# Pooled attention and a four-expert feed-forward in one kernel: weight loads by halves, four weight sums on GpSimd, one copy on ScalarE

## The chip, the core and the metric

The kernel runs on one core of one Trainium2 chip. A core has TensorE (PE, with its weight loads PEld), VectorE (DVE), ScalarE (ACT), GpSimd (POOL) and SyncE (SP), and 16 DMA engines. The metric is the device time of one execution in microseconds, the median over runs.

## The reference

Inputs are in float32: q, k and v (8 batches, 8 heads, 576 tokens, 64 channels), probabilities of 4 experts for each of 8 x 576 = 4608 tokens, and the experts' weights w1 (4 x 512 x 1024) and w2 (4 x 1024 x 512).

```python
k_p = k.reshape(B, H, 72, 8, D).mean(axis=3)      # keys and values averaged over 8 tokens
v_p = v.reshape(B, H, 72, 8, D).mean(axis=3)
attn = softmax(q @ k_p.T / sqrt(D))
x = (attn @ v_p) as (4608, 512)                   # heads side by side
p = probs / (probs.sum(-1) + 1e-9)
out = sum over e of p[:, e] * (relu(x @ w1[e]) @ w2[e])
```

Nearly all arithmetic is in the two products of each expert.

## The kernel before

**Chunks.** The tokens are cut into nine chunks of 512: the first 512 tokens of each batch, and a last chunk of the remaining 64 tokens of all eight. For each chunk the attention gives a turned input xT (512 channels by 512 tokens, bf16); then each expert has an up-product with w1, a relu into a hidden tile H, and a down-product with w2, whose parts are scaled by the probability and added to acc.

**Seven products for eight.** Most products are done by a scheme of seven block products with sums of blocks (Strassen's, in Winograd's form). `up_product(c, e, unit, step)` (L680, matmuls L698) does step 0 to 6 of an up-product for one of two units of columns, `down(c, e, step)` (L749, matmuls L766) a step of a down-product. They need sums of weight blocks, made once for each expert: `first_weight_sums(e)` gives four of w1 (three into the tile wu, one in place into w1's own tile), `weight_sums(e)` four of w2 (three into the tile wt, one in place). Each is one `combine` (L249, a tensor_tensor on VectorE over 128 x 1024 bf16 elements). Sums over a chunk's input are `x_sum` (tile xs and one in place), over its hidden tile `hidden_sums` (tiles S2, S3 and in place). Relu sums from PSUM (L678), evictions into acc (L842) and copies (L711, L713, L774 on ScalarE) drain the banks.

**The first chunk** is written out by hand in `first_chunk`, since weights are still arriving. Expert 0 is done first, expert 1's up-product plainly, and expert 1's and 2's down-products plainly by `down_plain` (L787, matmuls L792): for one block of 128 tokens eight matmuls of 128 x 512, the eight chunks of w2's rows in order, then one eviction. Between them stands the attention of chunk 1: `queries_of_two` turns queries on PE into a bank and copies them out (L374), `keys` does so for keys (L304, L306), `scores_of_two` makes scores (L388) and exponents (L399, L413), `values_folds` sums value rows on VectorE into vp (L275, L338), `context` multiplies by vp (L463) and divides (L424, L425), `turn` turns the result (L481, L483). `context` goes through the heads in order, and vp is filled by two halves of heads.

**Order.** Each engine runs its instructions in the order in which the program lists them, and waits on semaphores. Loads with a change of type from float32 to bf16 are issued from GpSimd's queue (`nc.gpsimd.dma_start`), in program order: after the first keys and values, w1 of experts 0 and 1, the probabilities, w1 of 2, w2 of 0, w1 of 3, keys, queries, w2 of 1, values, w2 of 2, and, inside `first_chunk`, w2 of 3 (which waits until its room, used for partial sums, is free) and the keys, queries and values of chunk 2 (`load_wide`, `load_q`, `load_q_rem`). The software queue has eight semaphores in turn, so a load is issued when the load eight places before it has landed.

The loads of the weights are these:

```python
def load_w1(e):
    n = 2 if e == 0 else 1          # column halves
def load_w2(e):
    n = 2 if e in (0, 2) else 1     # row halves
```

**From chunk 1 on** a loop over slots g takes one step of an up-product and one of the down-product of the expert before in each slot, with attention pieces of later chunks at listed slots. In its first slots the down-product is that of chunk 0 and expert 3, which uses wt of expert 3 from step 2 on. One part in seven of the down-products is added to acc on GpSimd (`POOLED`, L780, a tensor_tensor over 128 x 512 float32); otherwise GpSimd does no arithmetic after the start.

Of the kernel before, what the change touches and what calls it, by code (L numbers as in the profile page):

```python
# [10 lines left out]
ALU = mybir.AluOpType  # L11
# [6 lines left out]
def kernel(  # L18
# [10 lines left out]
    nc = tc.nc  # L29

    B, H, S, D = q.shape
    E, DM, F = moe_w1.shape
# [7 lines left out]
    KC = DM // P  # L40
# [16 lines left out]
    HF, HN, HD, HK = FCH // 2, NT // 2, DM // 2, KC // 2  # L57
# [9 lines left out]
    chains = [psum.tile([P, NT], F32, name=f"o_ps{i}") for i in range(2)]  # L67
# [81 lines left out]
    def rows_of(src, b, lo, hi):  # L149
        return src[b].rearrange("h (j r) d -> j h r d", r=POOL)[:, :, lo:hi, :]  # L150
# [13 lines left out]
    def load_wide(what, part):  # L164
        src, raw, wide = ((k, raw_k, wide_k), (v, raw_v, wide_v))[what]
        n = wide.shape[2]
        if part == 0:
            nc.gpsimd.dma_start(out=wide, in_=rows_of(src, BUSY, 0, n))
        else:
            n += 2 * (part - 1)  # L170
            nc.gpsimd.dma_start(out=raw[:], in_=rows_of(src, BUSY, n, n + 2),
                                accum_op=ALU.add if part > 1 else ALU.bypass)
# [30 lines left out]
        )  # L203

    def load_w1(e):
        n = 2 if e == 0 else 1
        for i in range(n):
            fs = slice(i * F // n, (i + 1) * F // n)

            for ks in [slice(0, HK), slice(HK, KC)] if n == 2 and i == 0 else [slice(0, KC)]:  # L210
                nc.gpsimd.dma_start(  # L211
                    out=w1_bf[:, e, ks, fs],
                    in_=moe_w1[e][:, fs].rearrange("(kc p) f -> p kc f", p=P)[:, ks],
                )

    def load_w2(e):
        n = 2 if e in (0, 2) else 1
        for i in range(n):
            fcs = slice(i * FCH // n, (i + 1) * FCH // n)
            nc.gpsimd.dma_start(  # L220
                out=w2_bf[:, e, fcs], in_=moe_w2[e].rearrange("(fc p) d -> p fc d", p=P)[:, fcs]
            )
# [23 lines left out]
            in1=inv[:].unsqueeze(2).to_broadcast([P, NBLK, E]), op=ALU.mult,  # L246
        )

    def combine(dst, a, op, b):  # L249
        nc.vector.tensor_tensor(out=dst, in0=a, in1=b, op=op)  # L250

    state = {}
    turns = {"spare": 0, "work": 0, "att": 0, "up": 0}
# [109 lines left out]
    def queries_of_two(pair, bank, copy):  # L363

        q_sb = raws[("q", 1)]
        if pair == 0:
            state[("qT", 1)] = apool.tile([P, H, 2, P], BF16, name="qT")
        qt_ps = bank.bitcast(BF16)[:, 0:8 * P].rearrange("p (h a t) -> p h a t", h=4, a=2)
        for hh in range(4):
            for rr in range(2):  # L370
                nc.tensor.transpose(
                    qt_ps[:, hh, rr, :], q_sb[:, 2 * pair + hh, 2 * rr:2 * rr + 2, :], ident[:]
                )
        copy(out=state[("qT", 1)][:, 2 * pair:2 * pair + 4], in_=qt_ps)  # L374
# [18 lines left out]
    def scores(b, pair, part=None):  # L393
        sc_ps = two_banks(b)
        if part != 1:
            score_products(b, pair, [sc_ps[:, r2] for r2 in range(2)])
        if part == 0:
            return
        nc.scalar.activation(  # L399
            out=state[("expT", b)][:, 2 * pair:2 * pair + 2].rearrange("j h a b t -> j b (h a) t"),  # L400
            in_=sc_ps[0:SP].rearrange("j b (h t) -> j b h t", t=P),
            func=ACT.Exp, scale=EXP_SCALE,
        )

    def scores_of_two(b, pair, bank=1):

        scores(b, pair, 0 if b > 1 else None)
        banks = [unit[bank][:] for unit in units]  # L410
        score_products(b, pair + 1, banks)
        for r2 in range(2):
            nc.scalar.activation(  # L413
                out=state[("expT", b)][:, 2 * pair + 2:2 * pair + 4, :, r2].rearrange("j h a t -> j (h a) t"),
                in_=banks[r2][0:SP].rearrange("j (h t) -> j h t", t=P),
                func=ACT.Exp, scale=EXP_SCALE,
            )
# [227 lines left out]
        w = w1_bf[:, e]  # L645
        return w[:, 0:HK, 0:FH], w[:, HK:KC, 0:FH], w[:, 0:HK, FH:F], w[:, HK:KC, FH:F]

    def first_weight_sums(e):
        b11, b21, b12, b22 = weight_parts(e)
        t = wu_bf[:, e]  # L650
        return [lambda: combine(t[:, 0], b12, ALU.subtract, b11),
                lambda: combine(t[:, 1], b22, ALU.subtract, t[:, 0]),
                lambda: combine(t[:, 2], b21, ALU.subtract, t[:, 1]),
                lambda: combine(b12, b22, ALU.subtract, b12)]

    def x_parts(c):

# [67 lines left out]
    def weight_sums(e):  # L725
        w, t = w2_bf[:, e], wt_bf[:, e]
        b11, b12 = w[:, LO, 0:HD], w[:, LO, HD:DM]
        b21, b22 = w[:, HI, 0:HD], w[:, HI, HD:DM]
        return [lambda: combine(t[:, 0], b12, ALU.subtract, b11),
                lambda: combine(t[:, 1], b22, ALU.subtract, t[:, 0]),  # L730
                lambda: combine(t[:, 2], b21, ALU.subtract, t[:, 1]),
                lambda: combine(b12, b22, ALU.subtract, b12)]

    def quarters(c, e):
# [52 lines left out]
    def down_plain(c, e, r, fcs=range(FCH)):  # L787
        H_sb = hidden[(c, e)]
        o_ps = chains[r % 2][:]
        for fc in fcs:  # L790
            lhs = H_sb[:, fc // HF, r // 2, fc % HF, (r % 2) * P:(r % 2 + 1) * P]
            nc.tensor.matmul(  # L792
                o_ps, lhsT=lhs, rhs=w2_bf[:, e, fc, :],
                start=(fc == 0), stop=(fc == FCH - 1), skip_group_check=True,
            )
        if fcs.stop == FCH:
            add(o_ps, c, e, r, slice(0, DM), True)
# [71 lines left out]
    def first_chunk():  # L869


        def each(*pieces):
            for piece in pieces:
                piece()

        sums = {e: first_weight_sums(e) for e in range(E)}

        def both(e, step):
            for unit in (1, 0) if e == 3 else (0, 1):
                up_product(0, e, unit, step)  # L880

        each(*(lambda n=n: x_sum(0, n) for n in range(4)), *sums[0][0:3])
        norm_probs()
        up(0, 1, (0, 1))
        hidden_sums(0, 0, 0)
        hidden_sums(0, 0, 1)
        up(0, 1, (2, 3))
        each(*sums[1][0:3])
        up(0, 1, (4,), bank=units[0][1][:])
        each(sums[2][0], sums[2][1], sums[2][3], sums[2][2])  # L890
        up(0, 1, (5,), bank=chains[0])
        both(2, 0)
        up(0, 1, (6,), bank=chains[1])
        both(2, 1)
        up(0, 1, (7,), bank=chains[0])
        last_sum = weight_sums(0)
        each(sums[0][3], sums[1][3], *last_sum[0:2])
        both(2, 2)
        down(0, 0, 0)
        both(2, 3)  # L900
        hidden_sums(0, 0, 2)
        down(0, 0, 1)
        both(2, 4)
        hidden_sums(0, 0, 3)
        down(0, 0, 2)
        both(2, 5)
        each(*last_sum[2:])
        down(0, 0, 3)
        both(2, 6)
        each(*sums[3][0:2])  # L910
        both(3, 0)
        down(0, 0, 4)
        both(3, 1)
        each(sums[3][3], sums[3][2])
        fold_keys(1)
        down(0, 0, 5)
        both(3, 2)
        down(0, 0, 6)
        both(3, 3)
        queries_of_two(0, att[:, 0], nc.scalar.copy)  # L920
        both(3, 4)
        both(3, 5)
        keys(1, every)
        queries_of_two(2, chains[0][:], nc.vector.tensor_copy)
        both(3, 6)
        load_w2(3)
        scores_of_two(1, 0, 0)
        rest = weight_sums(1)[0:3]
        each(*rest[0:2])
        down_plain(0, 1, 0)  # L930
        lo, hi = slice(0, H // 2), slice(H // 2, H)
        each(*values_folds(1, lo))
        scores_of_two(1, 2, 0)
        fold_first, *fold_rest = values_folds(1, hi)
        fold_first()
        down_plain(0, 1, 1)
        each(*fold_rest)
        load_wide(0, 0)
        load_q(2)
        load_wide(0, 1)  # L940
        load_q_rem(0)
        load_q_rem(1)
        load_wide(1, 0)
        load_wide(1, 1)
        load_wide(1, 2)
        down_plain(0, 1, 2)
        context(1, 0)
        rest[2]()
        down_plain(0, 1, 3)
        context(1, 1)  # L950
        turn(1, 0)
        hidden_sums(0, 3, 0)
        down_plain(0, 2, 0)
        context(1, 2)
        turn(1, 1)
        hidden_sums(0, 3, 1)
        down_plain(0, 2, 1)
        context(1, 3)
        turn(1, 2)
        each(*weight_sums(3)[0:3])  # L960
        down_plain(0, 2, 2)
        turn(1, 3)
        each(*(lambda n=n: x_sum(1, n) for n in range(3)))
# [67 lines left out]
    with tc.manual_schedule(  # L1031
# [31 lines left out]
        sums = {}  # L1063
# [4 lines left out]
        for g in range(7 * N + 1):  # L1068
            t, i = divmod(g, 7)
# [53 lines left out]
```

## Time and profile before

| | |
|---|---|
| median of 3 runs | 489.89 us (489.87 to 489.92) |
| span of the profiled execution | 488.7 us |
| what lies beside the span in an execution | 1.2 us (median less span; the page gives no other time of the profiled execution) |
| granted TensorE clock, mean | 0.998 |
| DMA | 41.98 MB, mean 86 GB/s, some 200 GB/s in the first 60 us |

Busy time is the sum of an engine's instructions and a share of the span. Matmuls are pipelined and their ends are modelled, so a busy PE is not PE at its peak. In the timeline each row is start, duration, engine, line, operation, output and inputs, shape and count; brackets give the idle time before and who ended it. In a table of stretches each pair is busy time and count for PE, PEld, DVE, ACT and POOL, then the clock, the DMA share and GB/s.

### The profile page before, as it was taken

Reading aid. Unit: us, or ns where it says so; the run is one execution under the profiler, and the core shown is the slowest. Engines: PE = TensorE matmul, PEld = TensorE weight load, DVE = VectorE, ACT = ScalarE, POOL = GpSimd, SP = SyncE. Lnnn points to the kernel's source line nnn. Section 1 sums busy time; section 2 is a strip of 40 time slices with the busy share of each in tenths; the row PEclk is TensorE's granted clock in tenths of the full one; section 3 lists DMA queues with packets and bytes.
Section 4 is the critical chain, followed back from the end, with each engine's and each line's share of the span. In section 5 each row is a group of like instructions: output and inputs, shape, how many; then the busy total and the mean of one; then the engine's idle time right before and its main releaser. Section 6 shows DMA issues by size and latency. Waiting matters only on the chain.

```text
span 488.7 us, 11602 instructions
## 1 busy us (share of the span) xinstructions
PE 480.9 (98%) x4717; PEld 412.2 (84%) x4721; DVE 378.9 (78%) x764; ACT 304.8 (62%) x583; POOL 118.4 (24%) x118
## 2 busy tenths in 40 slices
PE   8999999999999999999999999999999999999996
PEld 4868578898888888888889889888888888888885
DVE  5789899789768976797679866997678766876674
ACT  5787445855676567656765567556755567556650
POOL 8330504242523154016411442111011101110100
PEclk9999999999999999999999999999999999999999
DMA  9999999876966679345945296311112010004003
GB/s 198 209 205 203 201 180 136 99 89 63 113 101 57 88 80 144 34 82 59 160 48 90 27 169 62 68 23 66 34 23 23 23 65 3 12 23 86 1 1 88
DMA packets 101877, 41.98 MB, mean 86 GB/s; under 512 B 73904, under 2 KB 100272, under 8 KB 101824
## 3 DMA queue, kind: packets, MB, share of 16 engines
q0 software_dynamic: 56992, 22.42, 40.4%
q1 hardware_dynamic: 43728, 17.77, 16.7%
q10 hardware_dynamic: 1104, 1.05, 0.6%
q8 instruction: 37, 0.61, 0.5%
q14 instruction: 16, 0.13, 0.1%
HBM read 45.69 MB, written 9.44 MB: 113 GB/s over the span
## 4 chain that ended last, share of the span: by engine, by line
PE 89%; DMA 8%; POOL 2%; issue 0%; DVE 0%; POOLq 0%
PE unit L698 40%; PE o_ps L766 40%; DMA w_bf<-in_moe_w_dram 8%; PE o_ps L792 3%; PE att L463 2%; PE unit L825 1%; POOL wt_bf L144 1%; PE att L388 1%; PE unit L388 1%; POOL w_bf L211 0%; PE att L517 0%; PE att L500 0%; PE unit L481 0%; POOL q_sb L181 0%; PE o_ps L825 0%
## 5 line engine op out<-in xcount | busy, mean ns | idle before, releaser
L842 DVE SCALAR_TENSOR_TENSOR acc<-o_ps,p_all,acc 128x256 f32<-128x256 f32 (+1 forms) x285 | 127.0, 486 | 50.8 <-PE o_ps L766 36.6
L766 PEld LDWEIGHTS <-H 128*128 128x128 bf16 x1320 | 129.1, 98 | 15.0
L698 PEld LDWEIGHTS <-w_bf 128*128 128x128 bf16 x1088 | 105.1, 98 | 13.1 <-DMA w_bf<-in_moe_w_dram 0.4
L678 DVE CUSTOM_DVE_ANT_0 H<-unit,partial 128x512 bf16<-128x512 f32 x128 | 87.3, 685 | 26.4 <-PE unit L698 12.2
L766 PE MATMUL o_ps<-w_bf,H 128*128 128x256 bf16 x792 | 102.6, 273 | 0.0
L698 PE MATMUL unit<-xT,w_bf 128*128 128x256 bf16 x704 | 100.5, 273 | 0.0
L780 POOL TENSOR_TENSOR acc<-acc,addend 128x512 f32<-128x512 f32 x24 | 30.4, 1267 | 255.1 <-ACT addend L778 213.1
L713 ACT COPY partial<-unit 128x512 f32<-128x512 f32 x128 | 72.3, 592 | 30.3 <-PE unit L698 30.2
L698 PEld LDWEIGHTS <-wu_bf 128*128 128x128 bf16 x816 | 77.6, 98 | 11.6 <-issue 2.5
L698 PE MATMUL unit<-xs,wu_bf 128*128 128x256 bf16 x512 | 77.0, 273 | 0.0
L766 PE MATMUL o_ps<-wt_bf,H 128*128 128x256 bf16 x528 | 68.4, 273 | 0.0
L715 ACT ACTIVATE H<-unit 128x512 bf16<-128x512 f32 x66 | 39.8, 605 | 30.9 <-PE unit L698 30.9
L766 PEld LDWEIGHTS <-S 128*128 128x128 bf16 x528 | 51.7, 98 | 6.0
L719 ACT ACTIVATE H<-unit 128x512 bf16<-128x512 f32 x66 | 39.6, 602 | 25.6 <-PE unit L698 25.3
L711 ACT COPY unit<-unit 128x512 f32<-128x512 f32 x68 | 39.4, 582 | 23.6 <-PE unit L698 18.0
L698 PE MATMUL unit<-xs,w_bf 128*128 128x256 bf16 x256 | 38.4, 273 | 0.0
L840 ACT ACTIVATE acc<-o_ps,p_all 128x256 f32<-128x256 f32 x72 | 30.7, 485 | 9.4 <-PE o_ps L766 7.9
L698 PE MATMUL unit<-xT,wu_bf 128*128 128x256 bf16 x240 | 35.7, 272 | 0.0
L154 POOL DMA_DIRECT2D kraw<-in_k_dram x20 | 26.4, 1319 | 36.7 <-DMA kraw<-in_k_dram 36.7
L766 PE MATMUL o_ps<-wt_bf,S 128*128 128x256 bf16 x264 | 34.2, 273 | 0.0
L766 PE MATMUL o_ps<-w_bf,S 128*128 128x256 bf16 x264 | 34.2, 273 | 0.0
L154 POOL DMA_DIRECT2D vraw<-in_v_dram x20 | 29.1, 1454 | 20.4 <-DMA vraw<-in_v_dram 15.2
(157 smaller groups left out, 508.4 us busy)
## 6 DMA issues: line engine op xcount, KB each, us to landing
out_dram<-acc SPq DMA_DIRECT2D x32, 256.0 KB, 4.2
w_bf<-in_moe_w_dram POOLq DMA_DIRECT2D x5, 1024.0 KB, 15.6
q_sb<-in_q_dram POOLq DMA_DIRECT2D x7, 512.0 KB, 9.9
vraw<-in_v_dram POOLq DMA_DIRECT2D x22, 144.0 KB, 6.6
kraw<-in_k_dram POOLq DMA_DIRECT2D x21, 144.0 KB, 5.5
w_bf<-in_moe_w_dram POOLq DMA_DIRECT2D x5, 512.0 KB, 18.2
wt_bf<-in_k_dram POOLq DMA_DIRECT2D x4, 144.0 KB, 5.4
wt_bf<-in_v_dram POOLq DMA_DIRECT2D x4, 144.0 KB, 4.2
```

The lines of the kernel that those rows point to most:

```text
L154: nc.gpsimd.dma_start(out=raw[:], in_=rows_of(src, b, 2 * part, 2 * part + 2), accum_op=ALU.add if part else ALU.bypass)
L678: nc.vector._custom_dve(TENSOR_ADD_SAT, out=dst, in0=ps, in1=part, s0=LARGEST, s1=0.0)
L698: nc.tensor.matmul(ps[:, n * HN:(n + 1) * HN], lhsT=lhs[:, kc, f:f + P], rhs=rhs[:, kc, :], start=(not grows and n == 0 and kc == 0), stop ...
L711: nc.scalar.copy(out=banks[1][:], in_=ps)
L713: nc.scalar.copy(out=part[:, step - 2], in_=ps)
L715: nc.scalar.activation(out=quarter(0, 0), in_=ps, func=ACT.Relu)
L719: nc.scalar.activation(out=quarter(0, 1), in_=ps, func=ACT.Relu)
L766: nc.tensor.matmul(ps[:, j], lhsT=lhs[:, i, j * P:(j + 1) * P], rhs=rhs[:, i, :], start=(not grows and i == 0 and j == 0), stop=(i == HF - 1),
L780: nc.gpsimd.tensor_add(out=dst, in0=dst, in1=addend[:])
L792: nc.tensor.matmul(o_ps, lhsT=lhs, rhs=w2_bf[:, e, fc, :], start=(fc == 0), stop=(fc == FCH - 1), skip_group_check=True,)
L840: nc.scalar.activation(out=dst, in_=o_ps, func=ACT.Copy, scale=prob)
L842: nc.vector.scalar_tensor_tensor(out=dst, in0=o_ps, scalar=prob, in1=dst, op0=ALU.mult, op1=ALU.add,)
```

## The change

- The loads of w1 of experts 1 and 2 and of w2 of expert 1 are issued as two halves each (w1 by columns, w2 by rows); w2 of expert 2 has two halves before and after, the last expert's loads stay whole.
- In the first chunk the in-place sum of expert 3's w1 (`sums[3][3]`) goes to GpSimd and is listed directly after `sums[3][0]`, ahead of `sums[3][1]`.
- The first three sums of expert 3's w2 (`weight_sums(3)[0:3]`) go to GpSimd, and the load `load_wide(1, 2)` is listed behind them.
- The copy of the second half of chunk 1's turned queries goes from VectorE to ScalarE.
- Of expert 1's w2 sums the first is listed ahead of the scores of the first pair, the second behind the first plain down-product; before, both stood ahead of it.

```diff
@@ -203,18 +203,18 @@
         )
 
     def load_w1(e):
-        n = 2 if e == 0 else 1
+        n = 1 if e == E - 1 else 2
         for i in range(n):
             fs = slice(i * F // n, (i + 1) * F // n)
 
-            for ks in [slice(0, HK), slice(HK, KC)] if n == 2 and i == 0 else [slice(0, KC)]:
+            for ks in [slice(0, HK), slice(HK, KC)] if e == i == 0 else [slice(0, KC)]:
                 nc.gpsimd.dma_start(
                     out=w1_bf[:, e, ks, fs],
                     in_=moe_w1[e][:, fs].rearrange("(kc p) f -> p kc f", p=P)[:, ks],
                 )
 
     def load_w2(e):
-        n = 2 if e in (0, 2) else 1
+        n = 1 if e == E - 1 else 2
         for i in range(n):
             fcs = slice(i * FCH // n, (i + 1) * FCH // n)
             nc.gpsimd.dma_start(
@@ -246,8 +246,8 @@
             in1=inv[:].unsqueeze(2).to_broadcast([P, NBLK, E]), op=ALU.mult,
         )
 
-    def combine(dst, a, op, b):
-        nc.vector.tensor_tensor(out=dst, in0=a, in1=b, op=op)
+    def combine(dst, a, op, b, on=None):
+        (on or nc.vector).tensor_tensor(out=dst, in0=a, in1=b, op=op)
 
     state = {}
     turns = {"spare": 0, "work": 0, "att": 0, "up": 0}
@@ -645,13 +645,13 @@
         w = w1_bf[:, e]
         return w[:, 0:HK, 0:FH], w[:, HK:KC, 0:FH], w[:, 0:HK, FH:F], w[:, HK:KC, FH:F]
 
-    def first_weight_sums(e):
+    def first_weight_sums(e, late=None):
         b11, b21, b12, b22 = weight_parts(e)
         t = wu_bf[:, e]
         return [lambda: combine(t[:, 0], b12, ALU.subtract, b11),
                 lambda: combine(t[:, 1], b22, ALU.subtract, t[:, 0]),
                 lambda: combine(t[:, 2], b21, ALU.subtract, t[:, 1]),
-                lambda: combine(b12, b22, ALU.subtract, b12)]
+                lambda: combine(b12, b22, ALU.subtract, b12, late)]
 
     def x_parts(c):
 
@@ -726,9 +726,10 @@
         w, t = w2_bf[:, e], wt_bf[:, e]
         b11, b12 = w[:, LO, 0:HD], w[:, LO, HD:DM]
         b21, b22 = w[:, HI, 0:HD], w[:, HI, HD:DM]
-        return [lambda: combine(t[:, 0], b12, ALU.subtract, b11),
-                lambda: combine(t[:, 1], b22, ALU.subtract, t[:, 0]),
-                lambda: combine(t[:, 2], b21, ALU.subtract, t[:, 1]),
+        on = nc.gpsimd if e == E - 1 else nc.vector
+        return [lambda: combine(t[:, 0], b12, ALU.subtract, b11, on),
+                lambda: combine(t[:, 1], b22, ALU.subtract, t[:, 0], on),
+                lambda: combine(t[:, 2], b21, ALU.subtract, t[:, 1], on),
                 lambda: combine(b12, b22, ALU.subtract, b12)]
 
     def quarters(c, e):
@@ -873,7 +874,7 @@
             for piece in pieces:
                 piece()
 
-        sums = {e: first_weight_sums(e) for e in range(E)}
+        sums = {e: first_weight_sums(e, nc.gpsimd if e == E - 1 else None) for e in range(E)}
 
         def both(e, step):
             for unit in (1, 0) if e == 3 else (0, 1):
@@ -907,11 +908,11 @@
         each(*last_sum[2:])
         down(0, 0, 3)
         both(2, 6)
-        each(*sums[3][0:2])
+        each(sums[3][0], sums[3][3], sums[3][1])
         both(3, 0)
         down(0, 0, 4)
         both(3, 1)
-        each(sums[3][3], sums[3][2])
+        sums[3][2]()
         fold_keys(1)
         down(0, 0, 5)
         both(3, 2)
@@ -921,13 +922,14 @@
         both(3, 4)
         both(3, 5)
         keys(1, every)
-        queries_of_two(2, chains[0][:], nc.vector.tensor_copy)
+        queries_of_two(2, chains[0][:], nc.scalar.copy)
         both(3, 6)
         load_w2(3)
+        rest = weight_sums(1)[0:3]
+        rest[0]()
         scores_of_two(1, 0, 0)
-        rest = weight_sums(1)[0:3]
-        each(*rest[0:2])
         down_plain(0, 1, 0)
+        rest[1]()
         lo, hi = slice(0, H // 2), slice(H // 2, H)
         each(*values_folds(1, lo))
         scores_of_two(1, 2, 0)
@@ -942,7 +944,6 @@
         load_q_rem(1)
         load_wide(1, 0)
         load_wide(1, 1)
-        load_wide(1, 2)
         down_plain(0, 1, 2)
         context(1, 0)
         rest[2]()
@@ -958,6 +959,7 @@
         context(1, 3)
         turn(1, 2)
         each(*weight_sums(3)[0:3])
+        load_wide(1, 2)
         down_plain(0, 2, 2)
         turn(1, 3)
         each(*(lambda n=n: x_sum(1, n) for n in range(3)))
```

## The prediction, made before the changed kernel had run

> **What bounds the kernel now.** I read the page first, then the waits of PE, then the timeline around the one long wait, then the stretches after it.
>
> ```profile
> span 488.7 us, 11602 instructions
> PE 480.9 (98%) x4717; PEld 412.2 (84%) x4721; DVE 378.9 (78%) x764; ACT 304.8 (62%) x583; POOL 118.4 (24%) x118
> ```
>
> PE is busy for 98% of the span, so 7.8 us is idle. The waits of PE say where it is not start-up:
>
> ```profile
> PE o_ps L792 <- DMA w_bf<-in_moe_w_dram: 0.6, 1, 0.6
> ```
>
> It is the only wait above 0.4 us after the first matmul. The first plain down-product of expert 1 waits for the 1 MB load of its w2. The timeline from 48 us:
>
> ```profile
> 50.35 0.38 PE L388 MATMUL unit<-qT,kpT 64*128 64x256 bf16 x4
> 51.34 1.90 PE L792 MATMUL o_ps<-w_bf,H 128*128 128x512 bf16 x7 [0.61 <-DMA w_bf<-in_moe_w_dram]
> 51.39 0.69 DVE L250 TENSOR_TENSOR wt_bf<-w_bf 128x1024 bf16<-128x1024 bf16 x1 [0.15 <-DMA w_bf<-in_moe_w_dram]
> ...
> 52.12 0.69 DVE L250 TENSOR_TENSOR wt_bf<-w_bf,wt_bf 128x1024 bf16<-128x1024 bf16 x1
> ...
> 53.28 0.75 DVE L842 SCALAR_TENSOR_TENSOR acc<-o_ps,p_all,acc 128x512 f32<-128x512 f32 x1 [0.47 <-PE o_ps L792]
> ...
> 57.03 0.29 DVE L338 TENSOR_TENSOR vp<-wt_bf 72x256 bf16<-72x256 bf16 x1
> 57.18 0.48 PE L463 MATMUL att<-vp,expT 72*128 72x65 bf16 x8
> ```
>
> Two things: while PE waits, DVE does one of the two weight sums in its shadow; and at 57.18 PE is already level with DVE, since the second half of the context needs the vp that ends at 57.32 (its row is 0.48 where later ones are 0.42). Then the stretches:
>
> ```profile
> 50.00:55.00 5.00, 4.34 (x31) 1.92 (x31) 4.31 (x8) 3.38 (x5) 0.89 (x1) 1.00 1.23 199
> 65.00:70.00 5.00, 4.95 (x36) 3.36 (x36) 4.90 (x10) 2.12 (x4) 0.00 (x0) 1.00 1.72 178
> 70.00:75.00 5.00, 5.00 (x48) 4.49 (x46) 4.86 (x10) 3.12 (x7) 1.41 (x1) 1.00 1.17 158
> 75.00:80.00 5.00, 5.00 (x48) 4.47 (x47) 4.96 (x12) 2.76 (x6) 1.89 (x2) 1.00 0.89 113
> ```
>
> From 65 to 80 us both PE (first pair) and DVE (third) are full. From there to the end PE has no hole, so whatever PE loses or gains before 80 us stays in the time. The most the change can bring is the 0.6 us.
>
> **Halves.** Three more loads (w1 of experts 1 and 2, w2 of 1) cost three issues of some 0.8 us on POOL (rows L211, L220). POOL idles 17.05 us before 51.77, and the queue holds several megabytes, so they are hidden; without that cover a later landing would cost 0.8 us each. Each software-queue load waits for the one eight before it, so the last half of expert 2's w2 goes out behind w1 of expert 3 (about 40 us instead of 33.96); that half is needed only after 59.7. The bytes move at 207 GB/s (45 to 50 us), so the first half of w2 of expert 1 lands about 2.6 us before 51.3, at 48.7. PE, free at 50.73, uses four chunks of 0.22 of it until 51.6; the second half is there by 51.3. The 0.61 goes, and the products of w1 gain nothing: no PE wait of note stands there.
>
> **What is late next.** The evicting sum at 53.28 comes 1.94 after the product's start, so at 50.73 + 1.94 = 52.67. The order as built puts the second weight sum (now behind that eviction) in front of the value folds: 0.65 more. From eviction to the end of vp was 57.32 - 53.28 = 4.04, now 4.69: vp ends at 57.36 against 57.32. PE is again held there, and the 0.6 is gone: net 0.0, at best 0.1. The freed copy of turned queries (0.69 of DVE at 49.35) gives nothing there, since DVE then waits for PE. On ACT it is 1.04 (row L374 ACT at 47.18) behind the key copy ending 49.83: the scores' exponent moves from 50.56 to about 50.8, and the banks are wanted back at 52.6; hidden, up to 0.2 if not.
>
> **Sums on POOL: the price of one.** No bf16 sum runs on POOL in this trace. The nearest row:
>
> ```profile
> 78.11 1.27 POOL L780 TENSOR_TENSOR acc<-acc,addend 128x512 f32<-128x512 f32 x1 [3.90 <-ACT addend L778]
> ```
>
> By bytes 1024 bf16 cost the same 1.27, by elements 2.53. A POOL instruction over one column takes 0.10, so (1.27 - 0.10)/512 = 2.28 ns an element and 2.4 us for 1024; the one-input bf16 selection L108, 657 elements in 0.86, shows no rate that bf16 doubles. I take 2.4; DVE took 0.69.
>
> **Does DVE run beside it?** None of the 24 L780 rows has a DVE instruction with two SBUF inputs started inside it: only evictions, which read PSUM. The one such meeting is at the start:
>
> ```profile
> 4.84 0.50 DVE L250 TENSOR_TENSOR S<-S 64x648 bf16<-64x648 bf16 x1 [0.98 <-POOL S L108]
> 5.02 0.47 POOL masks.py:199 TENSOR_SCALAR_AFFINE_SELECT ident<-ident 128x128 bf16<-128x128 bf16 x1
> ```
>
> By the rate of L108 (1.31 ns) the 128 elements of the second need 0.17; it took 0.47 and ended 0.15 after DVE's sum. That fits a POOL that stood still until DVE was through, though a fixed overhead would read alike. Bounds: no cost at all, or each waits for the other's whole instruction. I take the second, as that row is the only one that bears on it.
> [...]
>
> **First sum on POOL** (w1 of expert 3): ready at 41.65, it goes behind DVE's sum that ends at 42.38, and runs to 44.8. DVE's third sum, 43.68 before, starts at 44.8, though the sum ahead of it (43.08) is no longer DVE's. PE's key turning at 48.44 needs the eviction that ended at 47.80, so 0.6 of lag is free and 0.5 remains, in the hole before 51.3 first, then at vp.
>
> **Three sums on POOL** (w2 of expert 3). This load is the shortest to land of its line, 12.3 us:
>
> ```profile
> DMA to landing us min/median/max: 12.3/21.3/25.9
> ```
>
> 51.77 + 12.3 = 64.1, a date that PE does not set, so it swallows the gains and losses before it. With 0.1 between instructions: first sum 64.2 to 66.6, second 66.7 to 69.1. DVE's x sums are wanted at 66.9 (ACT's turn copy ends at 66.88) and start at 69.1. The three of them take 1.2 (68.08 to 69.29 before), to 70.3; being back to back they leave POOL no gap. POOL's third sum goes into the eviction behind them, 70.4 to 72.8. The last x sum, 69.87 before, starts at 72.85: DVE is 3.0 late, in spite of the 2.1 of sums taken off it. The rows that follow it:
>
> ```profile
> 72.13 0.87 DVE L842 SCALAR_TENSOR_TENSOR acc<-o_ps,p_all,acc 128x256 f32<-128x256 f32 x2
> ...
> 74.37 1.04 PE L766 MATMUL o_ps<-wt_bf,H 128*128 128x256 bf16 x8
> 74.49 0.68 DVE L250 TENSOR_TENSOR w_bf<-w_bf 128x1024 bf16<-128x1024 bf16 x1
> ...
> 76.12 1.04 PE L766 MATMUL o_ps<-w_bf,S 128*128 128x256 bf16 x8
> ```
>
> The eviction ends at 73.00 + 3.0 and PE wants its bank at 74.37: 1.6 lost. The last weight sum ends at 75.17 + 3.0 = 78.2 and PE wants it at 76.12: 2.1 lost in all, the larger of the two. Later rows leave 1.2 or more to spare. Each 0.1 us on POOL's 2.4 is three times that in the end: 2.53 gives 2.5, 2.0 gives 0.9, 1.27 nothing. The load moved behind these sums (vraw, 72.81 before) goes out at about 73 and is folded after 82: hidden.
>
> **Sum.** The profiled span is 488.7; the median of 489.89 is 1.2 more, for what lies around it, which stays. 488.7 + 2.1 = 490.8, or 492.0 as a median.
>
> **Rivals.**
> No exclusion: DVE goes on beside POOL; then only the vp chain counts, 0.0 to -0.1: 489.8, not slower. For it: the trace shows no DVE row stretched by POOL. It decides once POOL's sum is under about 1.5 us or DVE's x sums do not wait. 0.22.
> Short exclusion: POOL's sum at 1.5 to 2.0, or the x sums get in ahead of its second: 0.2 to 0.9 lost, 490.4. 0.13.
> POOL between the x sums: its third sum takes the break after the first x sum, 69.6 to 72.0; the eviction behind them ends at 73.6, ACT's copy at 74.2, and PE's product of 70.88 starts at 74.3: 3.4 lost, 493.3. 0.08.
> Halves pay in full: vp is not what holds PE: 489.3. 0.05, as the row of 0.48 speaks against it.
> Forecast: 0.52.
>
> **How the numbers follow.** A difference of 0.2% is 0.98 us, about what a measurement of this kernel can tell from no change. Faster by that is beyond the 0.6 to be had: 0.02, for what the trace does not show. Slower: the forecast, the break case and an edge of the short one, 0.62. The rest, 0.36, is within. The range goes from the no-exclusion case with 0.3 to spare, 489.6, to just under the break case, 493.2; the forecast's own range is 490.9 to 492.6.
>
> **What would show it.** Right: no L792 wait near 51; POOL rows of 2.2 to 2.6 us at 42 and three from 64; a DVE x sum near 67 that starts late or is long; PE waits for DVE at L766 near 74 to 78. Wrong: DVE sums of 0.4 to 0.7 inside POOL's rows with PE full from 65 to 80, or POOL's sums near 1.3.

## The result, and the profile after

The changed kernel takes 492.83 us (median of 5 runs, 492.5 to 493.45), the kernel before on the same chip 489.91 (489.87 to 490.08): a ratio of 1.0061, 95% interval 1.005 to 1.0071. It is 2.9 us slower. The profiled execution took 492.5 us with a span of 490.7, so the times below explain a run at the fast end of the five. Predicted were 492.0 us and a span of 490.8; the median lies 0.8 above that, 0.2 beyond the forecast's own range (490.9 to 492.6) and 0.5 below the rival with POOL between the x sums (493.3).

The page, first line and busy times:

```profile
span 490.7 us, 11614 instructions
PE 481.2 (98%) x4721; PEld 412.3 (84%) x4721; DVE 379.7 (77%) x759; ACT 305.4 (62%) x584; POOL 129.7 (26%) x125
```

POOL has 11.3 us more. DVE, from which four sums and a copy were taken, has not less but 0.8 more: its remaining rows have become longer. That does not say where it hurts. The waits of PE do (line waited at, engine and line waited for, us, times, longest):

```profile
PE o_ps L767 <- ACT o_ps L775: 0.6, 1, 0.6
PE unit L698 <- DVE xs L250: 0.6, 1, 0.6
PE att L463 <- DVE vp L338: 0.6, 1, 0.6
```

The wait for w2 (L792 before, L793 now) is gone, and three of 0.6 have come. (Lines behind L726 have moved by one.) The stretches of after:

```profile
65.00:70.00 5.00, 5.00 (x38) 3.28 (x36) 4.25 (x4) 2.05 (x5) 4.84 (x3) 1.00 1.76 177
70.00:75.00 5.00, 3.78 (x34) 3.08 (x32) 4.96 (x10) 2.68 (x6) 1.94 (x2) 1.00 1.12 151
```

From 65 to 70 us DVE has 4 instructions where it had 10, in 4.25 us of busy time where it had 4.90: the third pair is full, but of waiting. From 70 to 75 PE issues 34 matmuls instead of 48. The timeline of after, first around the second half of the values:

```profile
50.78 1.89 PE L793 MATMUL o_ps<-w_bf,H 128*128 128x512 bf16 x8
52.76 0.75 DVE L843 SCALAR_TENSOR_TENSOR acc<-o_ps,p_all,acc 128x512 f32<-128x512 f32 x1 [1.08 <-ACT expT L413]
53.43 0.68 DVE L250 TENSOR_TENSOR wt_bf<-w_bf,wt_bf 128x1024 bf16<-128x1024 bf16 x1
57.12 0.29 DVE L338 TENSOR_TENSOR vp<-wt_bf 72x256 bf16<-72x256 bf16 x1
57.46 0.29 PE L463 MATMUL att<-vp,expT 72*128 72x65 bf16 x4 [0.56 <-DVE vp L338]
```

PE starts the down-product 0.6 earlier, has its eviction 0.5 earlier, and then waits 0.56 for vp, since the weight sum at 53.43 now stands between the eviction and the value folds. And then around the x sums, first three rows of before, then after:

```profile
68.08 0.41 DVE L250 TENSOR_TENSOR xs<-xT 128x512 bf16<-128x512 bf16 x1
68.53 0.43 DVE L250 TENSOR_TENSOR xs<-xs,xT 128x512 bf16<-128x512 bf16 x1
70.88 1.04 PE L766 MATMUL o_ps<-w_bf,H 128*128 128x256 bf16 x8
```

```profile
63.94 2.12 POOL L250 TENSOR_TENSOR wt_bf<-w_bf 128x1024 bf16<-128x1024 bf16 x1 [2.57 <-DVE S L250]
66.14 4.38 POOL L250 TENSOR_TENSOR wt_bf<-w_bf,wt_bf 128x1024 bf16<-128x1024 bf16 x2
67.00 1.55 DVE L250 TENSOR_TENSOR xs<-xT 128x512 bf16<-128x512 bf16 x1
68.58 2.22 DVE L250 TENSOR_TENSOR xs<-xs,xT 128x512 bf16<-128x512 bf16 x1
70.72 0.41 DVE L250 TENSOR_TENSOR xT<-xT 128x512 bf16<-128x512 bf16 x1
70.85 0.60 PE L698 MATMUL unit<-xs,wu_bf 128*128 128x256 bf16 x4 [0.60 <-DVE xs L250]
71.06 0.74 DVE L843 SCALAR_TENSOR_TENSOR acc<-o_ps,p_all,acc 128x512 f32<-128x512 f32 x1
71.89 0.57 ACT L775 COPY o_ps<-o_ps 128x512 f32<-128x512 f32 x1 [1.76 <-PE unit L698]
72.51 1.03 PE L767 MATMUL o_ps<-w_bf,H 128*128 128x256 bf16 x8 [0.62 <-ACT o_ps L775]
```

The third x sum, with nothing beside it, takes 0.41. The first took 1.55 and the second 2.22, and neither shows a bracket: a DVE instruction that stands still because of POOL is drawn as a long row, not as a wait. POOL's second sum, from 66.14, ends before the first x sum does, and its third, until 70.52, before the second x sum does. PE waits for the second x sum at 70.85, and the eviction listed behind the x sums ends at 71.80, so ScalarE's copy into that bank, and with it PE's product, come late at 72.51. (The copy's bracket names a product of PE that ended within 0.1 us of the eviction; in the kernel with the three sums alone, below, the same copy has DVE acc L843 there.)

Matched weight load by weight load, PE in after starts 0.63 earlier than before at 50.7, 0.08 later at 57.46, 0.85 later at 70.85, 1.63 later at 72.51, and from there the shift stays to the last matmul (483.66 before, 485.36 now). The last 0.3 of the span's 2.0 lies behind that. From the end of the last matmul to the end of the span it is 4.76 us here, 4.78 and 4.79 in two more profiles of this kernel, and 4.45 to 4.47 in all eight profiles of the kernel before and of the kernels with parts of the change. The last store lands 3.4 behind the last matmul in before and after alike; the 0.3 comes later, ahead of GpSimd's last semaphore instruction. Its cause stays open.

The first GpSimd sum:

```profile
41.79 2.62 POOL L250 TENSOR_TENSOR w_bf<-w_bf 128x1024 bf16<-128x1024 bf16 x1 [1.83 <-DVE wu_bf L250]
43.14 1.82 DVE L250 TENSOR_TENSOR wu_bf<-w_bf,wu_bf 128x1024 bf16<-128x1024 bf16 x1
```

Each held the other. POOL's 2.62 is 2.12 of work and 0.50 more, in which DVE's sum ahead, drawn to 42.43, was still running; DVE's 1.82 is 0.69 of work and 1.13 more, in which POOL's row ran, until 44.41. No wait of PE followed.

### The profile page after: what moved, and what is told of

Read it like the earlier page. It is cut to its first block, busy times and chain, and to the rows that moved or that the text cites. A ratio compares the mean times of both kernels' runs of the same rounds, so it can differ in the third digit from the quotient of the medians.

```text
span 490.7 us, 11614 instructions
## 1 busy us (share of the span) xinstructions
PE 481.2 (98%) x4721; PEld 412.3 (84%) x4721; DVE 379.7 (77%) x759; ACT 305.4 (62%) x584; POOL 129.7 (26%) x125
## 4 chain that ended last, share of the span: by engine, by line
PE 93%; DVE 2%; ACT 2%; POOL 1%; DMA 1%; issue 0%; POOLq 0%
PE unit L698 42%; PE o_ps L767 41%; PE att L463 1%; PE o_ps L793 1%; PE unit L826 1%; DMA wt_bf<-in_v_dram 1%; PE o_ps L617 1%; POOL wt_bf L144 1%; PE att L388 1%; PE unit L617 1%; DVE xs L250 1%; PE unit L634 1%; PE unit L388 0%; DVE wt_bf L275 0%; ACT qT L374 0%
## 5 line engine op out<-in xcount | busy, mean ns | idle before, releaser
L843 DVE SCALAR_TENSOR_TENSOR acc<-o_ps,p_all,acc 128x256 f32<-128x256 f32 (+1 forms) x285 | 127.0, 486 | 51.7 <-PE o_ps L767 36.3
L767 PEld LDWEIGHTS <-H 128*128 128x128 bf16 x1320 | 129.1, 98 | 15.8 <-issue 0.8
L767 PE MATMUL o_ps<-w_bf,H 128*128 128x256 bf16 x792 | 102.6, 272 | 0.6 <-ACT o_ps L775 0.6
L767 PE MATMUL o_ps<-wt_bf,H 128*128 128x256 bf16 x528 | 68.4, 273 | 0.0
L767 PEld LDWEIGHTS <-S 128*128 128x128 bf16 x528 | 51.7, 98 | 6.0
L767 PE MATMUL o_ps<-w_bf,S 128*128 128x256 bf16 x264 | 34.2, 273 | 0.0
L767 PE MATMUL o_ps<-wt_bf,S 128*128 128x256 bf16 x264 | 34.2, 273 | 0.0
```

Source lines behind the costliest of these rows:

```text
L767: nc.tensor.matmul(ps[:, j], lhsT=lhs[:, i, j * P:(j + 1) * P], rhs=rhs[:, i, :], start=(not grows and i == 0 and j == 0), stop=(i == HF - 1),
L843: nc.vector.scalar_tensor_tensor(out=dst, in0=o_ps, scalar=prob, in1=dst, op0=ALU.mult, op1=ALU.add,)
```

## The experiments

My theory after the result: VectorE's sums and GpSimd's sums exclude each other, and nearly all of the loss comes from the three w2 sums beside the x sums; the late second weight sum costs the 0.6 at vp, which the halves pay for. The rivals: the exclusion is not what holds DVE (the load moved behind the sums, or ScalarE, is), or the loss lies in the halves and the reordering.

**Which part costs it.** Four kernels, each one part of the change alone or taken back, with 6 to 11 runs each; the kernel before has 489.83 us beside them (29 runs).

*All but the three w2 sums on GpSimd.*

```diff
-        on = nc.gpsimd if e == E - 1 else nc.vector     # weight_sums, from after
+        on = nc.vector
```

> The whole change, but expert 3's three w2 sums stay on VectorE. Theory (these sums and VectorE's x sums exclude each other, and nothing else of the change costs): 489.8 to 490.1, no PE wait near 70.9 and 72.5, DVE x sums of 0.42 again, the PE wait of 0.6 at vp near 57.4 still there. Rival (the loads by halves, the first sum on GpSimd or the ScalarE copy bear the loss): 491 or more, with a PE wait elsewhere.

Measured: 490.56 us, ratio 1.0014 (1.0006 to 1.0023), profiled span 489.2. The x sums are back to 0.42, and both waits near 71 us are gone; the wait of 0.6 for vp stays, and this execution has one of 0.5 for expert 0's first weights at its start. Of the 0.61% of the whole change about 0.14% remain. The time is 0.5 us above the 490.1 expected at most, which fits halves that do not pay for the late vp (below).

*The three w2 sums on GpSimd alone*, with the load behind them:

```diff
-        load_wide(1, 2)                                 # before: behind load_wide(1, 1)
+        on = nc.gpsimd if e == E - 1 else nc.vector     # weight_sums: combine(..., on)
         each(*weight_sums(3)[0:3])
+        load_wide(1, 2)
```

> The kernel before, with only expert 3's three w2 sums on GpSimd and the load of vraw behind them. Theory: all of the loss is here, 491.4 to 493.4, with DVE x sums of 1.5 to 2.6 us and PE waits for xs or for the ScalarE copy of 0.6 or more between 69 and 78. Rival (the loss needs the earlier parts of the change, which shift PE against the landing of w2): under 490.3.

Measured: 492.49 us, ratio 1.0062 (1.0044 to 1.0081): the loss of the whole change, from this part by itself (six runs; two of them, at 494.09 and 495.09, make the interval wide). Its one new wait of PE and its timeline:

```profile
PE o_ps L767 <- ACT o_ps L775: 2.4, 1, 2.4
```

```profile
66.12 0.59 DVE L250 TENSOR_TENSOR xs<-xT 128x512 bf16<-128x512 bf16 x1
66.51 4.44 POOL L250 TENSOR_TENSOR wt_bf<-w_bf,wt_bf 128x1024 bf16<-128x1024 bf16 x2
66.74 2.23 DVE L250 TENSOR_TENSOR xs<-xs,xT 128x512 bf16<-128x512 bf16 x1
68.89 2.34 DVE L250 TENSOR_TENSOR xT<-xT 128x512 bf16<-128x512 bf16 x1
```

POOL's first sum, 64.30 to 66.42, let the first x sum go with 0.59; then the two engines take turns, sum for sum. The moved load is issued at 71.89 and nobody waits for it. Nor is the length of GpSimd's sums by itself what PE waits for: they end at 70.95, and the first product that reads them, at 72.62 in before, comes at 74.34 here. All the loss is in one place here, where it was in two in after, and here PE had lost nothing at vp: the two kernels come out alike, although after loses 0.6 more ahead of 60 us. GpSimd's sums start when the load has landed (64.30 here, 63.94 in after), so a PE that arrives later waits less. (The bracket of the first sum in after names a VectorE sum that ended at 63.92; the load had landed at 63.80, and in all five executions with this sum on GpSimd it starts 0.14 behind the landing.)

*The halves alone.*

```diff
-        n = 2 if e == 0 else 1                          # load_w1
+        n = 1 if e == E - 1 else 2
-        n = 2 if e in (0, 2) else 1                     # load_w2
+        n = 1 if e == E - 1 else 2
```

> The kernel before, with only the loads by halves. Theory (vp is late in the changed kernel because the second weight sum stands behind the eviction; here both sums run from 51.3 to 52.7, ahead of the eviction at 52.7): the 0.6 of the PE wait is won, 489.2 to 489.4, with vp done near 56.7. Rival (vp holds PE whatever the order): 489.8 to 490.0 with a PE wait of 0.5 or more for vp.

Measured: 489.86 us, ratio 1.0 (0.9992 to 1.0009). A miss: the 0.6 that the profile before showed was not won. In this kernel PE does not wait for w2, but, as the single executions below show, neither did the kernels with the whole load in three of four.

*The halves, and expert 1's second w2 sum behind the down-product:*

```diff
-        scores_of_two(1, 0, 0)
         rest = weight_sums(1)[0:3]
-        each(*rest[0:2])
+        rest[0]()
+        scores_of_two(1, 0, 0)
         down_plain(0, 1, 0)
+        rest[1]()
```

> As the halves alone, with expert 1's w2 sums in the order of the changed kernel (the second behind the first plain eviction). Theory: vp ends near 57.4 and PE waits for it by 0.5 to 0.7, 489.8 to 490.0. Rival (the order costs nothing): the same time as the halves alone, 489.3.

Measured: 490.29 us, ratio 1.0006 (0.9998 to 1.0015), 0.43 us more than the halves alone, and 0.3 above what was expected, as the halves alone were 0.5 above. PE waits 0.5 for vp (L463), which it does not in the halves alone. So the reordering seems to cost some 0.4 us, in the place where it was expected.

**The rest of the change, and how the exclusion works.** In a second set (the kernel before at 489.94 us):

*All but the w2 sums on GpSimd and the reordering:* the first kernel above with the old order of expert 1's sums. What is left of the change are the halves, the first sum on GpSimd and the copy on ScalarE.

```diff
-        rest = weight_sums(1)[0:3]
-        rest[0]()
         scores_of_two(1, 0, 0)
+        rest = weight_sums(1)[0:3]
+        each(*rest[0:2])
         down_plain(0, 1, 0)
-        rest[1]()
```

> The whole change without the three w2 sums on GpSimd and with expert 1's w2 sums in the order of before; so loads by halves, the first sum on GpSimd and the copy on ScalarE are left. Theory (the order cost 0.5 at vp, the rest nothing): 489.7 to 490.1 and no PE wait for vp. Rival (the first sum on GpSimd or the ScalarE copy cost 0.3 or more): 490.2 to 490.6 with a PE wait between 44 and 54 or one at vp again.

Measured: 490.12 us, ratio 1.0001 (0.9992 to 1.001), no wait for vp. DVE's third w1 sum is again held, 1.82 from 43.01, and it costs nothing that can be measured. Against the first kernel of all, 490.56, the reordering is again 0.44 us of median, or 0.55 with each kernel taken against the kernel before of its own set.

*The first of the three w2 sums alone on GpSimd.*

```diff
-        return [lambda: combine(t[:, 0], b12, ALU.subtract, b11),
+        return [lambda: combine(t[:, 0], b12, ALU.subtract, b11, on),   # on: GpSimd for expert 3
```

> The kernel before with only the first of expert 3's three w2 sums on GpSimd, the other two on VectorE behind it, vraw behind. Theory (the loss is the meeting with the x sums; this one ends near 66.2, before them, and VectorE's other two end near 67.5 as before): 489.7 to 490.3, x sums of 0.42. Rival (any bf16 sum on GpSimd costs some 0.9 us): 490.6 or more.

Measured: 490.48 us, ratio 1.0007 (0.9995 to 1.0019). GpSimd's sum runs from 63.98 to 66.10, ahead of the x sums, which keep 0.41 and 0.42. But DVE's second sum reads its result and idles 1.57 until 66.13, and PE loses 0.5 at L767. Even with no meeting of the two engines, 0.69 us of VectorE's work cost 2.12 on GpSimd, and the chain of the sums is longer by the difference. The time falls between the theory's 490.3 and the rival's 490.6, for a reason that neither named. The load of vraw is moved here too, and the x sums are not held: the moved load is not what holds them.

*The exclusion by itself:* a small program without the kernel's work, in which GpSimd and VectorE run listed numbers of instructions from a common start.

```diff
+ ([pool_sum] * 4, [])                         # 128x1024 bf16, two SBUF inputs
+ ([], [dve_sum] * 6)
+ ([pool_sum] * 4, [dve_sum] * 12)             # all into one tile
+ ([pool_sum] * 4, [dve_free] * 12)            # each into a tile of its own
+ ([pool_sum] * 4, [dve_evict] * 12)           # reads PSUM and one SBUF input
+ ([pool_sum] * 4, [dve_copy] * 16)            # bf16, SBUF to SBUF
+ ([pool_set] * 10, [dve_sum] * 8)             # GpSimd only writes
```

> Not the reference's computation at all: GpSimd and VectorE instructions on fixed tiles in seven stretches. Theory (exclusion of two-SBUF-input instructions for whole instructions, taking turns): a GpSimd sum of 1024 bf16 takes 2.1 alone and a VectorE sum 0.7 alone; beside each other VectorE's sums wait up to 2.1 and only some five run beside four GpSimd sums, the GpSimd rows are 2.1 to 2.9; evictions that read PSUM keep their length beside GpSimd sums; VectorE sums beside GpSimd memsets keep 0.7. Independent VectorE sums without a wait between them: prediction's step says that they leave GpSimd no gap (GpSimd starves until they end, some 8 us), the traces of the change say that it gets its turn after one. Rival (they share bandwidth): both kinds stretch by a factor in every row. [...]

Alone, a GpSimd sum takes 2.12 us and VectorE's 0.69. The groups of lines of this program, in the stretch with sums on both engines and in the one with evictions (count, then busy us and mean ns of one):

```profile
L59 DVE TENSOR_TENSOR vo<-va,vb 128x1024 bf16<-128x1024 bf16 x12 | 15.5, 1290 | 1.0 <-ACT vb L49 0.6
L53 POOL TENSOR_TENSOR po<-pa,pb 128x1024 bf16<-128x1024 bf16 x4 | 10.0, 2494 | 6.0 <-ACT vb L49 5.8
```

```profile
L65 DVE SCALAR_TENSOR_TENSOR fo<-bank,res,fa 128x512 f32<-128x512 f32 x12 | 9.0, 750 | 1.1 <-ACT fa L50 0.7
L53 POOL TENSOR_TENSOR po<-pa,pb 128x1024 bf16<-128x1024 bf16 x4 | 8.5, 2121 | 6.2 <-ACT pb L48 6.0
```

Twelve VectorE sums took 15.5 us instead of 8.3: four of them were drawn at 2.49, that is one for each GpSimd sum, and the other eight at 0.69. With outputs in tiles of their own, so that no sum waits for the one ahead of it, it is the same (GpSimd 2.49 in the mean, VectorE's held rows 2.60). So a row of back-to-back VectorE sums did not keep GpSimd out; after each one GpSimd got its turn (its four sums were through in 10.2 us, VectorE's twelve in 15.0). Evictions go on at 0.75 and GpSimd at 2.12. VectorE's bf16 copies, with one input, are held as well: 2.22 beside sums, 0.43 alone. The memsets of the last stretch did not wait for its start and ran beside the rest of the copies, which took 1.13 there; the sums of that stretch then ran alone.

*What GpSimd does, and how long:* the same program with other operations.

```diff
+ ([pool_set] * 10, [dve_free] * 12)
+ ([pool_half] * 4, [dve_sum] * 10)            # GpSimd: 128x512 bf16
+ ([pool_wide] * 4, [dve_evict] * 16)          # GpSimd: 128x512 float32
+ ([pool_wide] * 4, [dve_sum] * 10)
```

> Not the reference's computation: GpSimd and VectorE instructions on fixed tiles. Theory (two SBUF inputs on VectorE meet GpSimd only where that one reads SBUF): VectorE sums beside GpSimd memsets keep 0.69 and the memsets 0.95; beside GpSimd sums of 512 bf16 (1.1 to 1.3 by themselves) each VectorE sum waits one of them, 1.7 to 2.0 a row; beside float32 sums of 512 (1.27, the form that the kernel has had all along) evictions keep 0.75 and VectorE sums are held to 1.9 to 2.2. Rival (a memset excludes as well, as it did VectorE's copies): VectorE sums of 1.4 to 1.7 beside memsets.

Measured: beside GpSimd's memsets VectorE's sums keep 0.68. A GpSimd sum of 512 bf16 elements is drawn at 1.48 beside VectorE's sums, and those at 1.52, both some 1.0 less than with 1024. The float32 sum of 512 takes 1.27 with evictions beside it, which stay at 0.75; beside VectorE sums it is drawn at 1.72 and they at 1.63 to 1.73. The held rows are shorter than expected (1.7 to 2.0, and 1.9 to 2.2): the hold follows the length of GpSimd's instruction, but is some 0.3 us shorter (2.49 - 0.69 = 1.80 beside a sum of 2.12, 1.63 - 0.69 = 0.94 beside one of 1.27). VectorE's sums were held beside GpSimd's sums, which read SBUF (rows of 1.52 to 2.60), and not beside its memsets, which read nothing (0.68).

**Single executions again**, one profile each.

> The kernel before, once more with a profile, since its runs here spread over 489.5 to 490.8 and the run with the w2 sums on GpSimd alone had no wait for w2 of expert 1 though it loads it whole. [...] Rival (the wait is always 0.6 and the halves win it): a wait of 0.5 to 0.7 again.

The kernel before, again: 490.32 us, span 488.6. PE reaches the down-product at 51.17, w2 has landed at 51.13, and there is no wait for it. Nor is there one in the two other kernels profiled that load this w2 whole (the three sums alone, the first sum alone). Of four executions with whole loads only the one of the page before shows the 0.61. The second execution is no faster for it: its PE had lost 0.7 at the start (L314, waiting for the values' load; 0.2 in the first) and came to its scores at 50.59, not 50.12, and to the down-product when w2 was just in. In the two other kernels w2 landed at 50.51 and 50.08, as PE came or before. So the landing spreads over 1.2 us, and the wait is there only when it falls behind PE. What sets the landing's date was not shown.

> The changed kernel once more, for its spread of 492.5 to 493.5. Theory (who gets a turn first between GpSimd's second and third sum and VectorE's x sums depends on when w2 of expert 3 lands against PE's progress, within some 0.5 us): VectorE and GpSimd rows alternate again without overlap of their work, the order differs from the first profile or its dates do by 0.2 to 0.6, PE loses 1.4 to 2.6 between 66 and 80. Rival (the spread is start-up alone): the same order and 1.6 lost again, with PE later by 0.3 or more already at 20 us.

> As the run before it, the same theories: 1.4 to 2.6 lost between 66 and 80 in an order that differs, or 1.6 again and a difference at 20 us.

The changed kernel again: 492.53 us with a span of 490.8, in the same order of turns as in the first profile, and 493.08 with a span of 491.2, in another. The timeline of the latter:

```profile
66.74 0.43 DVE L250 TENSOR_TENSOR xs<-xT 128x512 bf16<-128x512 bf16 x1
66.84 4.56 POOL L250 TENSOR_TENSOR wt_bf<-w_bf,wt_bf 128x1024 bf16<-128x1024 bf16 x2
69.35 2.34 DVE L250 TENSOR_TENSOR xT<-xT 128x512 bf16<-128x512 bf16 x1
```

GpSimd's first sum came 0.7 later (64.65), so the first x sum slipped in at 0.43 ahead of its second, and the second and third x sum were held instead. PE then loses 2.2 in one piece at L767. In the two executions PE's product starts at 72.60 and 73.06, that is 8.71 and 8.55 behind the landing of the load (63.89 and 64.51). So the 0.5 us between them is the date of the landing, and the other order of turns takes back 0.16. That this is also what spreads the five timed runs from 492.5 to 493.45 is argued, not shown.

## Why the prediction was right, and where

**The two engines exclude each other for whole instructions: right**, with three sums on GpSimd the largest term. Ahead of the result a single row of before bore on it (0.47 us at 5.02); what the runs showed is a VectorE sum 1.80 us longer beside a GpSimd sum of 2.12. The rival without exclusion is refuted by the rows of 1.55 and 2.22 and by the small programs: in them a VectorE sum with two SBUF inputs was held beside a GpSimd sum (2.49 against 0.69), and not beside memsets, which only write (0.68); an eviction from PSUM was not held (0.75). The bf16 copies, with one SBUF input, were held (2.22 against 0.43); the prediction does not consider them. (The 24 GpSimd rows of before that the prediction read have, besides evictions, seven relu sums started inside them; these read PSUM too and took 0.68, so the reading stands.)

**"Being back to back they leave POOL no gap": wrong.** GpSimd took its turn after each x sum. So the three sums of x neither waited until 69.1 nor ran together; the course was, in kind, that of the rival "POOL between the x sums", which had been given a chance of 0.08. PE was late at 70.85 and 72.51, not at 74.37 and 76.12.

**The price of one sum: mis-sized**, 2.12 us where 2.4 was taken from the float32 row. By the prediction's own rule of three, 2.1 - 3 x 0.28 = 1.3 us would have been lost by its course, and by the rival's 3.4 - 3 x 0.28 = 2.6. The traces show 1.55 in the first profile of after (0.85 - 0.08, and 1.63 - 0.85) and about 2.4 in the kernel with these sums alone. That the 2.1 was near in size is luck: a wrong order and a price too high made up for each other.

**Halves, and vp takes it back: right in the profiled execution** (vp's end at 57.36 predicted, 57.41 found; PE's shift there 0.08). **Wrong for the median.** The step that failed is "the median of 489.89 is 1.2 more, for what lies around it, which stays". The 50 timed runs of the kernel before in the two sets have 1.66 to 1.86 us outside their span and a median span of 488.1. By these the page before, with its span of 488.7, belongs to an execution of about 488.7 + 1.7 = 490.4 us (an estimate; its own time is not on record), half a microsecond above the median, and its 0.61 wait for w2 is about that much. Against a usual execution the halves win nothing (ratio 1.0). From the median span the prediction's sum would have been 488.1 + 2.1 + 1.7 = 491.9. What is missing to 492.83 shows beside the kernel with the halves alone, whose profile is of a median run (489.86, span 487.9): PE's product starts there at 70.08 and in after at 72.51, so 2.4 are lost and not 2.1, and 0.3 more lies behind the last matmul.

**"0.5 remains" of the first sum on GpSimd: nothing remained.** DVE's third sum ended at 44.96, earlier than the 45.5 that a start at 44.8 gave, and the keys were turned at 48.45 against 48.44. The kernel with that sum, the copy on ScalarE and the halves is at 1.0001.

**The date of the last load swallows what comes before it: right**, for what PE loses after 51.6. After, 0.6 late at vp, and the kernel with the three sums alone, not late there, have PE 0.9 apart at the x sums' stage (66.18 and 65.30, first product of the slots), but their held product starts at 72.51 and 72.60, and their last matmul ends at 485.96 and 485.99. In the four executions with three sums on GpSimd that product starts 8.4 to 8.7 behind the landing. "A date that PE does not set" goes too far, though: the load is issued when ScalarE's first exponents end (51.63 in after), and these wait for PE's scores.

**Still open:** the ratios of the parts beside the three sums have intervals of about 0.1% to either side, so an effect below 0.5 us of the halves, the ScalarE copy or the first sum isn't excluded; the ScalarE copy was never run by itself. The 0.4 of the reordering rests on two differences of medians whose intervals overlap, and on the wait of 0.5 to 0.6 that every trace with it shows.

## What to carry to other kernels

Before a sum is moved to an idle GpSimd, list the VectorE instructions with two SBUF inputs that run in the same stretch: each of them can be held once for most of a GpSimd instruction, here 1.8 us beside a sum of 2.12 that VectorE does in 0.69, so what is taken off VectorE's list comes back as longer rows. Here bf16 copies from SBUF to SBUF belong on that list too (2.22 us against 0.43). If the stretch holds evictions from PSUM alone, which kept their 0.75 here, the move is free of that, but whoever waits for the sum still gets it 1.4 us later. And before a single wait of a profile is counted as time to be had, put that execution's span and what lies around it against the span of the timed runs: a wait that one execution in four shows need not be in the median.

## What the runs showed of the hardware

- VectorE and GpSimd sums over SBUF alternate one for one, also when VectorE's are queued back to back without a wait between them (held rows of 2.49 to 2.60 us, GpSimd rows of 2.44 to 2.65, against 0.69 and 2.12 alone). In these runs neither engine starves.
- The hold is drawn inside the row of the held instruction. The views of waits do not show it; the count of instructions in a stretch does (4 where 10 were, from 65 to 70 us). The row is longer by some 0.3 us less than GpSimd's instruction: by 1.80 beside 2.12, by 0.94 beside 1.27.
- VectorE's bf16 copy from SBUF to SBUF, with a single input, is held too: 2.22 us beside GpSimd's sums, 1.13 beside its memsets, 0.43 alone, though the same memsets leave VectorE's sums at 0.68.
- A GpSimd sum of 128 x 1024 bf16 takes 2.12 us, and the float32 one of half as many elements 1.27.
